# The first x tile of a gated SSM/MLP kernel: two of its five slabs by a plain load and TensorE transposes, three by one DMA transpose

## Chip, cores and metric

The kernel runs on one core of one Trainium2 chip. The metric is device microseconds (us) of one execution, the median of several runs. All tensors in memory are bf16.

## What is computed

`x` has 2048 rows of 640 features. Two branches read it and a gate mixes them.

```
g = sigmoid((x * gate_w).sum(-1))              # one number a row
a = 2 * Re(C h_t) + x * Dskip                  # h_t = Lam_bar * h_(t-1) + B_bar x_t, complex, 640 states
b = gelu(x @ w1 + b1) @ w2 + b2                # 640 -> 1728 -> 640
out = g * a + (1 - g) * b
```

`Lam_bar` and `B_bar` come from `Lambda`, `log_dt` and `B`, all per state. The recurrence over 2048 rows is done by the kernel in blocks of 256 rows.

## The kernel before

**Tiles.** The 2048 rows are cut into four x tiles of 512 rows. Products that contract over features need x with features on the partitions: `xT[q]` is `[128, 5, 512]`, five slabs of 128 features each. Gate and skip need the rows on the partitions: `xn` is `[128, 4, 640]`, two buffers used in turn. Before the change every `xT` comes by a DMA transpose out of memory (`xtrans`, L345, by `load_T`, L328, whose DMA is issued at L332) and every `xn` by a plain load (`xnload`, L336, by `load`, L323, whose DMA is issued at L325).

**Stages on TensorE.** For each x tile: the first MLP product (`m1_first` for the first eight hidden blocks of tile 0, L598; `m1` for all others, L618; a tail of 64 hidden units, L636), the SSM input product (`bproj`, L658), and per 128 rows the second MLP product (L745, tail L759) and the SSM output product (`cproj`, L791). ScalarE empties the PSUM banks (GELU at L607, L625 and L645, copies at L667, L773, L802). VectorE builds the SSM's tables at the start (L460, fed by `cols`), then scans (L698), computes the gates (L575) and combines (L460, L810).

**The opening.** `m1_first` (L591) runs slab by slab over the features: k = 0 for hidden blocks 0 to 6, then k = 1 for blocks 0 to 6, the left-over k = 0 of block 7 and k = 1 of block 7, then k = 2, 3 and 4 for all eight blocks. That is 40 matmuls of 128x128 by 512, all eight PSUM banks open at once. A matmul of slab k needs slab k of `xT[0]` and block k of W1 (`w1_k`, 128 rows by 1024 columns, 256 KB). Block 0 of W1 is loaded from ScalarE's queue, the others from SyncE's (SP's). Ahead of them TensorE runs a warm-up of eight matmuls on a zeroed tile `wz` (L400), which VectorE clears (L393).

A small transpose `cols` on TensorE (L410) turns 29 rows of parameters into columns. Everything that VectorE does for the SSM's tables starts from its copy (`cols1`, L415). It needs the identity matrix `ident`, which VectorE makes out of an iota of GpSimd (L383 to L386).

**What sets the order.** Each operation is given to a planner (`Sched.order`, L43) with an engine, an assumed duration, dependencies by name and a priority; lower goes first among those that the planner takes for ready. The result is one fixed order for each engine, and the emitter adds the semaphore waits. Operations on SP have no dependencies except the stores, so SP issues its loads in the order of `prio`: at the start the DMA transpose of slab 0, that of slabs 1 and 2, W1 blocks 1 and 2, the transpose of slabs 3 and 4, W1 blocks 3 and 4, the rest of W1 (`w1_r`), then B (two transposes), `xT[1]`, `gwb`, `xn[0]`, W2 and so on.

Of the kernel before, what the change touches and what calls it, by code (L numbers as in the profile page):

```python
# [9 lines left out]
BF16 = mybir.dt.bfloat16  # L10
# [137 lines left out]
class Prog:  # L148
# [8 lines left out]
    def op(self, name, eng, dur, reads, writes, fn, prio=None, lat=0.0, after=()):  # L157
        deps = {}
        for k in reads:
            for w in self.last_w.get(k, ()):  # L160
                deps[w.idx] = w
        for k in writes:
            for w in self.last_w.get(k, ()):
                deps[w.idx] = w
            for r in self.last_r.get(k, ()):
                deps[r.idx] = r
        for a in after:
            deps[a.idx] = a
        deps = list(deps.values())
        E = self.E  # L170

        def run(eg, deps=deps, eng=eng, fn=fn):
            E.wait(eng, *[d.done for d in deps if not (eng == "pe" and d.eng == "pe")])
            return fn()

        it = self.sch.add(name, eng, dur, deps, run, prio=prio, lat=lat)
        for k in writes:
            self.last_w[k] = [it]
            self.last_r[k] = []
        for k in reads:  # L180
            self.last_r.setdefault(k, []).append(it)
        return it


def bass_gated_mix__ssm_conv_s5__dense_activation_gelu__prompt_kernel(
# [18 lines left out]
    _, S, D = A_x.shape  # L204
# [3 lines left out]
    KD = D // 128  # L208
# [13 lines left out]
    x2 = A_x[0]  # L222
# [3 lines left out]
    with ExitStack() as es:  # L226

        def SB(name, shape, dt):
            return es.enter_context(nc.sbuf_tensor(name, list(shape), dt))

        xT = [SB(f"xT_{i}", [128, KD, 512], BF16) for i in range(NQ)]
        xn = [SB(f"xn_{i}", [128, 4, D], BF16) for i in range(2)]
# [9 lines left out]
        cols = SB("cols", [128, 3 * KP + NF], FP32)  # L242
# [10 lines left out]
        ident = SB("ident", [128, 128], BF16)  # L253
# [33 lines left out]
        PS = [es.enter_context(nc.psum_tensor(f"ps{i}", [128, 512], FP32)) for i in range(8)]  # L287
# [13 lines left out]
        op = pr.op  # L301

        def inc(eng, ins):
            return E.inc(eng, ins, eng + "_s")

        def dma_inc(eng, ins, sem):
            SEM(sem)
            E.count.setdefault(sem, 0)
            ins.then_inc(sems[sem], 16)
            E.count[sem] += 16  # L310
            return (sem, E.count[sem])
# [11 lines left out]
        def load(name, eng, sem, dst, src, writes, prio, dur=0.5, lat=2.5, reads=(), **kw):  # L323
            def fn():
                return dma_inc(eng, engines[eng].dma_start(dst, src), sem)  # L325
            return op(name, eng, dur, reads, writes, fn, prio=prio, lat=lat)

        def load_T(name, sem, pairs, writes, prio, dur, lat=3.0):  # L328
            def fn():
                t = None  # L330
                for dst, src in pairs:
                    t = dma_inc("sp", nc.sync.dma_start_transpose(dst, src), sem)  # L332
                return t
            return op(name, "sp", dur, (), writes, fn, prio=prio, lat=lat)

        def xnload(q, eng, prio=None):  # L336
            load(f"xn{q}", eng, f"l_xn{q}", xn[q % 2][:, :, :],
                 x2[q * 512:(q + 1) * 512, :].rearrange("(c p) d -> p c d", p=128),
                 [("xn", q % 2, 0), ("xn", q % 2, 1)], prio, dur=1.0, lat=6.0)
# [5 lines left out]
        def xtrans(q, ks, prio, dur):  # L345
            load_T(f"xT{q}_{ks[0]}", f"l_xT{q}_{ks[0]}", [(xT[q][:, ks[0]:ks[-1] + 1, :], x2[q * 512:(q + 1) * 512, ks[0] * 128:(ks[-1] + 1) * 128])],
                   [("xT", q, k) for k in ks], prio, dur)

        def w1load(k, eng, prio):
            load(f"w1_{k}", eng, f"l_w1{k}", W1sb[:, k, 0:FW], B_w1[k * 128:(k + 1) * 128, 0:FW], [("w1", k)], prio=prio, lat=2.6)  # L350

        w1load(0, "act", -101)
        xtrans(0, [0], 0, 1.27)
        xtrans(0, [1, 2], 1, 1.27)
        w1load(1, "sp", 2)
        w1load(2, "sp", 3)
        xtrans(0, [3, 4], 4, 1.27)
        w1load(3, "sp", 5)
        w1load(4, "sp", 6)
        load("w1_r", "sp", "l_w1r", W1sb[:, :, FW:F], B_w1[:, FW:F].rearrange("(k p) f -> p k f", p=128), [("w1", "r")], prio=20, lat=5.0)  # L360

        ROWS = {"lre": (0, A_Lambda_re), "lim": (KP, A_Lambda_im), "ldt": (2 * KP, A_log_dt), "b1a": (3 * KP, B_b1[0:nmain])}
# [24 lines left out]

        op("const", "dve", 0.8, ["iota"], ["ident"], f_const, prio=-65)

        wz = SB("wz", [128, 512], BF16)  # L390

        def f_wz():
            return inc("dve", nc.vector.memset(wz[:, :], 0.0))  # L393

        op("wz", "dve", 0.35, (), ["wz"], f_wz, prio=-70)

        def f_warm():
            t = None
            for _ in range(8):
                t = nc.tensor.matmul(PS[6][:, :], wz[:, 0:128], wz[:, :], start=True, stop=True)  # L400
            return inc("pe", t)

        op("warm", "pe", 3.2, ["wz"], [("bank", 6)], f_warm, prio=-1000)

        XT = {q: [("xT", q, k) for k in range(KD)] for q in range(NQ)}

# [2 lines left out]
        def f_cols():  # L409
            return inc("pe", nc.tensor.transpose(psC, rows[:, :], ident[:, :]))  # L410

        op("cols", "pe", 0.3, list(ROWS) + ["b1b", "ident"], [("bank", 7)], f_cols, prio=7.5)

        def f_cols1():
            return inc("dve", nc.vector.tensor_copy(out=cols[:, :], in_=psC[:, 0:RT + 1]))  # L415
# [129 lines left out]
            load_T(f"B{ci}", f"l_B{ci}", [(BT[:, ci, :, :], src)], [("BT", ci)], prio=30 + ci, dur=4.1)  # L545
        xtrans(1, range(KD), 32, 3.4)
        load("gwb", "sp", "l_gwb", gwb[:, :], gate_w.partition_broadcast(128), ["gwb"], prio=32.2)
        xnload(0, "sp", prio=32.4)
        load("w2a", "sp", "l_w2a", W2sb[:, 0:NF - 1, :], B_w2[0:nmain, :].rearrange("(j p) d -> p j d", p=128), ["w2a"], prio=33, lat=8.0)
        load("w2b", "sp", "l_w2b", W2sb[0:FL, NF - 1, :], B_w2[nmain:F, :], ["w2b"], prio=34, lat=4.0)  # L550
        load("w2c", "sp", "l_w2c", W2sb[64:64 + FL, NF - 1, :], B_w2[nmain:F, :], ["w2c"], prio=34.2, lat=4.0)
# [396 lines left out]
```

## Time and profile before

| What | Value |
|---|---|
| Median of 3 runs | 214.99 us (214.9, 214.99, 215.65) |
| Profiled execution | 215.15 us, of it the span of the profile 213.8 us |
| TensorE (PE) busy | 210.0 us, 98% of the span |
| VectorE (DVE) busy | 188.3 us, 88% |
| ScalarE (ACT) busy | 112.9 us, 53% |
| Read from memory, written | 7.63 MB, 2.62 MB |
| First matmul of the warm-up | 1.20 us |
| First and last matmul of `m1_first` (L598) | starts 4.82 us; the next stage's first (L618) starts 14.51 us |

Times in the profile count from the start of the span. PE is a matmul, PEld the load of its weights, SPq and ACTq the queues in which those engines issue DMAs; L12 is line 12 of the kernel. The time of a DMA issue in the timeline is the time that the queue spent on issuing; when the data landed is a number of its own. A matmul's duration includes its way through the array, and consecutive ones overlap: the distance from one start to the next tells the rate.

### The profile page before, as it was taken

Reading aid. Unit: us, or ns where it says so; the run is one execution under the profiler, and the core shown is the slowest. Engines: PE = TensorE matmul, PEld = TensorE weight load, DVE = VectorE, ACT = ScalarE, POOL = GpSimd, SP = SyncE. Lnnn points to the kernel's source line nnn. Section 1 sums busy time; section 2 is a strip of 40 time slices with the busy share of each in tenths; the row PEclk is TensorE's granted clock in tenths of the full one; section 3 lists DMA queues with packets and bytes.
Section 4 is the critical chain, followed back from the end, with each engine's and each line's share of the span. In section 5 each row is a group of like instructions: output and inputs, shape, how many; then the busy total and the mean of one; then the engine's idle time right before and its main releaser. Section 6 shows DMA issues by size and latency. Waiting matters only on the chain.

```text
span 213.8 us, 3098 instructions
## 1 busy us (share of the span) xinstructions
PE 210.0 (98%) x1257; PEld 119.3 (56%) x1257; DVE 188.3 (88%) x260; ACT 112.9 (53%) x205; POOL 2.5 (1%) x10
## 2 busy tenths in 40 slices
PE   7999999999999999999999999999999999999995
PEld 2344444444567675444467767444446777677673
DVE  1599999999999899999999999499999999988612
ACT  2569556679525334557835332556786554535230
POOL 1000000000000100000000010000000000000000
PEclk9999999999999999999999999999999999999999
DMA  7999699999000140000000023000000010000011
GB/s 138 297 271 192 142 364 271 224 191 204 0 0 3 61 153 3 31 0 0 0 3 31 0 49 138 32 0 0 3 0 2 0 34 31 31 34 31 31 34 31
DMA packets 30874, 16.35 MB, mean 76 GB/s; under 512 B 23948, under 2 KB 29964, under 8 KB 30860
## 3 DMA queue, kind: packets, MB, share of 16 engines
q1 hardware_dynamic: 30368, 14.57, 28.7%
q0 software_dynamic: 288, 1.31, 2.0%
q10 hardware_dynamic: 204, 0.27, 0.5%
q8 instruction: 10, 0.16, 0.4%
q14 instruction: 4, 0.03, 0.0%
HBM read 7.63 MB, written 2.62 MB: 48 GB/s over the span
## 4 chain that ended last, share of the span: by engine, by line
PE 95%; DMA 2%; SPq 1%; DVE 0%; issue 0%
PE ps L745 26%; PE ps L618 22%; PE ps L791 21%; PE ps L658 20%; PE ps L598 3%; DMA W1sb<-in_B_w_dram 2%; PE ps L759 1%; SPq L332 1%; PE ps L636 1%; DVE osb L824 0%
## 5 line engine op out<-in xcount | busy, mean ns | idle before, releaser
L745 PE MATMUL ps<-W2sb,Gl 128*128 128x320 bf16 x416 | 59.1, 299 | 0.0
L745 PEld LDWEIGHTS ps<-W2sb,Gl 128*128 128x128 bf16 x416 | 40.6, 98 | 16.5 <-ACT Gl L625 0.4
L618 PE MATMUL ps<-xT,W1sb 128*128 128x512 bf16 x220 | 48.1, 379 | 0.0
L791 PE MATMUL ps<-CT,H 128*128 128x320 bf16 x320 | 46.1, 299 | 0.0
L698 DVE TENSOR_TENSOR_SCAN W<-atab,V 128x1280 bf16<-128x1280 f32 x16 | 44.3, 2811 | 0.3
L658 PE MATMUL ps<-xT,BT 128*128 128x512 bf16 x200 | 43.8, 379 | 0.0
L773 ACT ACTIVATE E<-ps,g1col 128x320 bf16<-128x320 f32 x32 | 16.1, 526 | 42.2 <-PE ps L759 18.3
L791 PEld LDWEIGHTS ps<-CT,H 128*128 128x128 bf16 x320 | 30.7, 98 | 13.5 <-issue 1.8
L618 PEld LDWEIGHTS ps<-xT,W1sb 128*128 128x128 bf16 x220 | 21.5, 98 | 25.9
L625 ACT ACTIVATE Gl<-ps,cols 128x512 bf16<-128x512 f32 x44 | 29.7, 691 | 11.5 <-PE ps L618 11.5
L658 PEld LDWEIGHTS ps<-xT,BT 128*128 128x128 bf16 x200 | 19.4, 98 | 23.5 <-ACT Gl L625 0.4
L667 ACT ACTIVATE U<-ps 128x512 bf16<-128x512 f32 x40 | 23.6, 595 | 15.7 <-PE ps L658 15.6
L802 ACT ACTIVATE E<-ps,gcol 128x320 bf16<-128x320 f32 x30 | 15.7, 528 | 16.7 <-PE ps L791 16.6
L732 ACT ACTIVATE ps<-b2b 128x320 f32<-128x320 bf16 x32 | 14.0, 440 | 0.9
L460 DVE TENSOR_TENSOR osb<-xg,E 128x640 bf16<-128x640 bf16 x15 | 7.3, 487 | 7.8 <-ACT E L802 6.8
L810 DVE SCALAR_TENSOR_TENSOR xg<-xn,gcol,dsk 128x640 bf16<-128x640 bf16 x16 | 13.8, 882 | 0.4
L575 DVE SCALAR_TENSOR_TENSOR scr<-xn,gwb 128x640 bf16<-128x640 bf16 x16 | 13.2, 823 | 0.4
L460 DVE TENSOR_TENSOR H<-H,V 128x1280 bf16<-128x1280 bf16 x16 | 12.5, 821 | 0.3
L460 DVE TENSOR_TENSOR V<-V,W 128x1280 bf16<-128x1280 bf16 x16 | 12.5, 821 | 0.3
L460 DVE TENSOR_TENSOR V<-mr,U 128x2560 bf16<-128x2560 bf16 x8 | 11.9, 1489 | 0.2
L460 DVE TENSOR_TENSOR H<-c,W 128x2560 bf16<-128x2560 bf16 x8 | 11.9, 1488 | 0.1
L460 DVE TENSOR_TENSOR V<-s,W 128x2560 bf16<-128x2560 bf16 x8 | 11.9, 1484 | 0.0
(77 smaller groups left out, 101.2 us busy)
## 6 DMA issues: line engine op xcount, KB each, us to landing
out_dram<-osb SPq DMA_DIRECT2D x15, 160.0 KB, 1.8
W2sb<-in_B_w_dram SPq DMA_DIRECT2D x1, 2080.0 KB, 12.2
xn<-in_A_x_dram SPq DMA_DIRECT2D x2, 640.0 KB, 6.4
xn<-in_A_x_dram POOLq DMA_DIRECT2D x2, 640.0 KB, 4.8
W1sb<-in_B_w_dram SPq DMA_DIRECT2D x4, 256.0 KB, 4.1
W1sb<-in_B_w_dram SPq DMA_DIRECT2D x1, 880.0 KB, 6.1
W1sb<-in_B_w_dram ACTq DMA_DIRECT2D x1, 256.0 KB, 2.8
gwb<-in_gate_w_dram SPq DMA_DIRECT2D x1, 160.0 KB, 5.2
```

What stands on the lines that cost most here:

```text
L460: return inc("dve", nc.vector.tensor_tensor(out=o, in0=a, in1=b, op=o_))
L618: t = nc.tensor.matmul(PS[bank][:, :], W1sb[:, k, jf * 128:(jf + 1) * 128], xT[q][:, k, :], start=(k == 0), stop=(k == KD - 1))
L625: return inc("act", nc.scalar.activation(Gl[q % 2][:, jf, :], PS[bank][:, :], ACT.Gelu_apprx_tanh, bias=b1col[:, jf:jf + 1]))
L658: t = nc.tensor.matmul(PS[bank][:, :], BT[:, ci, kd, k * 128:(k + 1) * 128], xT[q][:, kd, :], start=(kd == 0), stop=(kd == KD - 1))
L667: return inc("act", nc.scalar.activation(dst, src, ACT.Copy, scale=1.0 if ci == 0 else -1.0))
L698: t = inc("dve", nc.vector.tensor_tensor_scan(out=g[:, ci, :], data0=a, data1=v[:, ci, :], initial=0.0, op0=ALU.mult, op1=ALU.add))
L732: return inc("act", nc.scalar.activation(PS[bank][:, 0:HALF], b2b[:, cols], ACT.Copy))
L745: t = nc.tensor.matmul(PS[bank][:, 0:HALF], Gl[q % 2][:, jf, t4 * 128:(t4 + 1) * 128], W2sb[:, jf, cols], start=False, stop=False, skip_gr ...
L773: return inc("act", nc.scalar.activation(E1[c % NE][:, cols], PS[bank][:, 0:HALF], ACT.Copy, scale=g1col[:, c:c + 1]))
L791: t = nc.tensor.matmul(PS[bank][:, 0:HALF], H[b % NHB][:, ci, k, s * 128:(s + 1) * 128], CT[:, ci, k, cols], start=(i == 0), stop=(i == 2 ...
L802: return inc("act", nc.scalar.activation(E2[c % NE][:, cols], PS[bank][:, 0:HALF], ACT.Copy, scale=gcol[:, c:c + 1]))
L810: return inc("dve", nc.vector.scalar_tensor_tensor(out=xg[c % 2][:, :], in0=xn[q % 2][:, c % 4, :], scalar=gcol[:, c:c + 1], in1=dsk[:, :] ...
```

## The change

Slabs 0 and 1 of the first x tile no longer come by DMA transpose. A plain load `xna` on SP brings their 256 features, rows on the partitions, into the first 256 columns of `xn[0]`. TensorE transposes them, four 128x128 blocks to a slab (`xt0`, `xt1`, into banks 7 and 6 as bf16), and VectorE copies each result into `xT[0]` (`xc0`, `xc1`). Slabs 2 to 4 come by one DMA transpose, now behind W1 blocks 1 and 2. The later load of `xn[0]` brings only the other 384 features (`xnb`).

The warm-up becomes six matmuls instead of eight, on a constant 1.0 read with stride 0 that exists before the kernel starts, so that `wz` and its clearing fall away. One more matmul on that constant with 192 columns (`fill`) stands behind the transposes. `cols` goes behind the ninth matmul of `m1_first` by priority (9.5), where it was behind the seventh (7.5).

```diff
+        KN = 2
         w1load(0, "act", -101)
-        xtrans(0, [0], 0, 1.27)
-        xtrans(0, [1, 2], 1, 1.27)
-        w1load(1, "sp", 2)
-        w1load(2, "sp", 3)
-        xtrans(0, [3, 4], 4, 1.27)
-        w1load(3, "sp", 5)
-        w1load(4, "sp", 6)
+        load("xna", "sp", "l_xna", xn[0][:, :, 0:KN * 128], x2[0:512, 0:KN * 128].rearrange("(c p) d -> p c d", p=128), ["xna"], 0, dur=0.5, lat=2.0)
+        w1load(1, "sp", 1)
+        w1load(2, "sp", 2)
+        xtrans(0, range(KN, KD), 3, 1.8)
+        w1load(3, "sp", 4)
+        w1load(4, "sp", 5)
...
-        wz = SB("wz", [128, 512], BF16)
-
-        def f_wz():
-            return inc("dve", nc.vector.memset(wz[:, :], 0.0))
-
-        op("wz", "dve", 0.35, (), ["wz"], f_wz, prio=-70)
+        one = nc.const_aps.tensor(1.0, [128, 1], BF16)

         def f_warm():
             t = None
-            for _ in range(8):
-                t = nc.tensor.matmul(PS[6][:, :], wz[:, 0:128], wz[:, :], start=True, stop=True)
+            for _ in range(6):
+                t = nc.tensor.matmul(PS[5][:, :], one.broadcast_to([128, 128]), one.broadcast_to([128, 512]), start=True, stop=True)
             return inc("pe", t)

-        op("warm", "pe", 3.2, ["wz"], [("bank", 6)], f_warm, prio=-1000)
+        op("warm", "pe", 2.5, (), [("bank", 5)], f_warm, prio=-1000)
+
+        for k in range(KN):
+            bank = 7 - k
+            pt = PS[bank][:, :].bitcast(BF16)[:, 0:512]
+
+            def f_xt(k=k, pt=pt):
+                t = None
+                for c in range(4):
+                    t = nc.tensor.transpose(pt[:, c * 128:(c + 1) * 128], xn[0][:, c, k * 128:(k + 1) * 128], ident[:, :])
+                return inc("pe", t)
+
+            op(f"xt{k}", "pe", 0.44, ["xna", "ident"], [("bank", bank)], f_xt, prio=-990 + k)
+
+            def f_xc(k=k, pt=pt):
+                return inc("dve", nc.vector.tensor_copy(out=xT[0][:, k, :], in_=pt))
+
+            op(f"xc{k}", "dve", 0.42, [("bank", bank)], [("xT", 0, k)], f_xc, prio=-2000 + k)
+
+        def f_fill():
+            return inc("pe", nc.tensor.matmul(PS[5][:, 0:192], one.broadcast_to([128, 128]), one.broadcast_to([128, 192]), start=True, stop=True))
+
+        op("fill", "pe", 0.16, (), [("bank", 5)], f_fill, prio=-980)
...
-        op("cols", "pe", 0.3, list(ROWS) + ["b1b", "ident"], [("bank", 7)], f_cols, prio=7.5)
+        op("cols", "pe", 0.3, list(ROWS) + ["b1b", "ident"], [("bank", 7)], f_cols, prio=9.5)
...
-        xnload(0, "sp", prio=32.4)
+        load("xnb", "sp", "l_xnb", xn[0][:, :, KN * 128:D], x2[0:512, KN * 128:D].rearrange("(c p) d -> p c d", p=128),
+             [("xn", 0, 0), ("xn", 0, 1)], 32.4, dur=1.0, lat=6.0, reads=["xna"])
```

## The prediction

> **What bounds the kernel now.** I read the chain of work that ended last first, then its pieces in order of time. The page gives the chain's shares:
>
> ```profile
> PE 95%; DMA 2%; SPq 1%; DVE 0%; issue 0%
> ```
>
> The chain in order of time shows where it is not TensorE:
>
> ```profile
> 2.03 1.29 SPq L332
> 3.32 0.05 issue
> 3.37 3.89 DMA W1sb<-in_B_w_dram
> 7.26 0.14 issue
> 7.39 7.28 PE ps L598 x33
> 14.67 5.40 PE ps L618 x25
> ...
> 211.61 0.55 DVE osb L824
> ```
>
> From 7.39 us on it is matmuls without a gap until the last copy. What ends last before that is the landing of W1 block 1, issued at 3.37 because two transpose issues stand ahead of it on SP. So the opening alone can move, and each us by which L618 starts earlier or later is a us of the whole. The timeline of the opening:
>
> ```profile
> 0.87 0.27 DVE L393 MEMSET wz<- 128x256 uint32 x1 [0.87 <-PEq L933]
> ...
> 1.20 3.59 PE L400 MATMUL ps<-wz 128*128 128x512 bf16 x8 [1.20 <-DVE wz L393]
> ...
> 4.82 2.13 PE L598 MATMUL ps<-xT,W1sb 128*128 128x512 bf16 x7
> 5.22 0.15 PEld L598 LDWEIGHTS ps<-xT,W1sb 128*128 128x128 bf16 x1 [0.27 <-issue]
> 5.65 0.81 PEld L598 LDWEIGHTS ps<-xT,W1sb 128*128 128x128 bf16 x4 [0.28 <-issue]
> ...
> 6.79 0.22 PE L410 MATMUL ps<-ident,rows 128*128 128x128 bf16 x1
> 7.04 0.19 DVE L415 CAST cols<-ps 128x29 f32<-128x29 bf16 x1 [5.12 <-PE ps L410]
> ...
> 7.39 6.85 PE L598 MATMUL ps<-xT,W1sb 128*128 128x512 bf16 x31 [0.39 <-DMA W1sb<-in_B_w_dram]
> ```
>
> Two facts matter. Of the gap only 0.39 us is idle: seven matmuls fill 4.82 to 7.0. And weight loads stand 0.43 us apart (5.22, 5.65) until about 5.65, where matmuls also last 609 to 634 ns and afterwards 379; later 65 matmuls take 14.03 us, 0.216 each. So TensorE runs at half rate until 5.65.
>
> **What the Trainium skill says.** "TensorE: Matmul & The Clock Gate", Part 1, says the array starts at half clock and is released after sustained activity in a free-running window of about 3.4 us, typically some 4 us after the start, varying by run. The trace agrees in kind: first matmul 1.20, full rate 5.65, 4.45 us. The same page, Part 4, gives a 128x128 bf16 transpose 275 to 390 ns singly and says that transposes do not count as busy for the clock in the same way; the one transpose here took 219 ns, at full clock, and about its weight for the clock the trace says nothing. "DMA: Bandwidth & Descriptors", "Issuing engines are not separate DMA queues": SP's and ACT's DMAs share 16 engines and interleave. The trace agrees: between 2.5 and 3.0 us both queues move data, 0.05 and 0.10 MB.
>
> **The change part by part.**
>
> *Warm-up without `wz`.* The 0.27 us clearing and its wait go. SP and ACT issue first at 0.75, GpSimd at 0.74, so TensorE starts near 0.8. Six matmuls at 0.43 end near 3.4.
>
> *`xna`.* It is issued at 0.75 and lands at L. W1 block 0, of the same 256 KB and issued at the same moment, landed after 2.8 us, at 3.55, alone; its packets ran from about 1.75 to 3.15. Now both loads share the engines. W1's 128 packets took 139 ns each there (49 packets at 84.7% of 16 engines in 0.5 us), 84 ns later in deep queues; `xna` has 512 pieces of 512 B. Packets of 256 B took 18 to 22 ns; I estimate 30 for 512 B. Together (128 x 84 to 139 + 512 x 30)/16 = 1.6 to 2.1 us after 1.75, and 0.4 to the semaphore: L = 3.8 to 4.2. I take 3.9; ends 3.55 (not disturbed at all) and 4.3.
>
> *Transposes and copies.* The old slab landed at 4.75 and TensorE began at 4.82: 0.07. A cold weight load is 0.15, a quarter of a cold matmul is 0.107: I take 0.13 a transpose, and 0.25 for the first load and way through the array beyond that: 4 x 0.13 + 0.25 = 0.77 for `xt0`, bounds 0.6 and 1.0. VectorE starts 0.03 behind (7.01 to 7.04). The copy of 512 columns out of PSUM isn't in the trace. 29 columns took 0.19 and 320 (two operands, f32) 0.55, so 0.19 + 483 x 1.24 ns = 0.79 is above it; half that slope gives 0.49. I take 0.55, bounds 0.45 and 0.75. TensorE again 0.05. `m1_first` starts at S = 3.9 + 0.07 + 0.77 + 0.03 + 0.55 + 0.05 = 5.37. `xt1` (0.52) and `fill` (0.16) stand inside `xc0`'s time. `xc1` ends about 0.6 after S, wanted by the seventh matmul. Both copies lie in VectorE's idle 5.12 us ahead of L415.
>
> *SP's queue.* Three transposes with 1.23 + 1.29 + 1.23 us of issue become one load (0.5) and one transpose, which I put at 1.6: two slabs cost 1.23 to 1.29, five under a full queue 4.61. W1 block 1 is issued at 1.25 instead of 3.37. Before, SP's 1.70 MB up to W1 block 4 flowed from 2.5 to about 10.1 us, 224 GB/s. At that rate, from 1.75, with W1 block 0's 0.26 MB ahead of all: W1 block 1 lands by 5.7 (wanted near 7.0), slabs 2 to 4 by 7.4 to 8.6 (wanted near 9.1), W1 block 4 by about 10.9 at worst (wanted near 12.5). So the old bound is gone and TensorE itself is next. The issue of B and everything behind it (`w1_r`, `xT[1]`, `xnb`, W2, C) comes up to 1.9 us earlier. `xnb` and `xna` carry together what `xn[0]` did; the added wait of `xnb` is for a landing some 18 us past: nothing.
>
> *`cols` at place nine.* It used to hide in the gap; now it costs 0.1 in the stream (0.05 to 0.2). It runs at about 7.4 instead of 6.79, so VectorE's tables are 0.65 later. What waits for that: the GELU table load, ended 11.23, then 11.9, with the first GELU wanted near 12.9; and the last state block, whose slack the end of the timeline shows:
>
> ```profile
> 197.72 1.56 DVE L460 TENSOR_TENSOR H<-H,V 128x1280 bf16<-128x1280 bf16 x2
> ...
> 202.43 2.89 PE L791 MATMUL ps<-CT,H 128*128 128x320 bf16 x20
> ```
>
> It is ready at 199.28 and used at 202.43: 3.15 us, far more than 0.65 plus the gain. If that cover were gone, the delay would count in full.
>
> *The sum.* With full clock at 5.65 as before: 0.28 us from S are at half rate, 0.65 of a matmul; the other 39.35 at 0.216 take 8.50; plus `cols` 0.1: L618 starts at 14.25. Before it was 7.39 + 33 x 0.216 = 14.52, which agrees with its 14.51. Gain 0.26 us. The profiled execution (213.8 span and 1.35 around it, 215.15) would become 214.89; it lies 0.16 above the median, so the median becomes 214.73, and I say 214.7. With all good ends (L 3.55, 0.6, 0.45) S is 4.75 and the gain 0.58; with all bad ends (4.3, 1.0, 0.75, 0.2) S is 6.2 and the loss about 0.55. This case's own range is 214.4 to 215.5.
>
> The removal sounds larger than it is: W1 block 1 comes 2 us earlier, but the seven half-clock matmuls under that wait were useful work, and now they start later.
>
> **Rivals.**
>
> *The clock comes late (slower).* The place is TensorE between the warm-up's end at 3.4 and S. There it idles about 0.5 us and then only transposes for about 1.2 us. Before, it was busy all of 1.20 to 5.65. If that stretch fails the activity test, the release waits for another window, 5.65 + 3.41 (the page's figure) = 9.06 at worst. Then 3.69 us from S hold 8.6 matmuls, 31.4 take 6.78, `cols` 0.1: L618 at 15.94, a loss of 1.4, 216.4 us. For: the skill's sentence on transposes, and the shorter warm-up. Against: a window which is half full may do, and `fill` and the weight loads also work the array. Each us of delay past S costs 0.49 us (1 - 0.216/0.43); it is a loss from about 6.2 and passes 0.5% from about 8.1. A release halfway, at 7.3, gives 215.5.
>
> *The clock comes early (faster).* TensorE starts 0.4 us sooner. If release follows the start, or comes at the least time of 3.4 us, it is there by 4.3 to 5.2. With L at 3.55 and S at 4.75 all 40 matmuls run full: 4.75 + 8.64 + 0.1 = 13.49, gain 1.0, 214.0 us. Against: everything must go well.
>
> *The slabs are late.* If three slabs in one transpose take longer than the bytes say (the first two calls before issued 393 KB at 0.75 and landed it at 5.83), k = 2 waits at 9.1 for a landing near 10, 215.6 us. Against: a slack of 0.5 to 1.7. That the change does not do what it says is hardly possible here: the priorities alone order SP's first loads.
>
> **How the numbers follow.** Likeliest case 0.58 (214.7), late clock 0.22 (216.4 in full, 215.5 halfway), early clock 0.14 (214.0), late slabs 0.06 (215.6). A measurement of this kernel tells about 0.5%, 1.07 us, from no change: below 213.9 is faster, above 216.1 slower. Slower gets a little over half of the late clock, 0.12, and 0.01 of the slabs. Faster gets a third of the early clock, 0.05. The rest, 0.82, is within. The range leaves out those ends, 0.18: 213.9 to 216.1.
>
> **What would show it.** Right: the first warm-up matmul near 0.8; transposes near 4.0; L598 from about 5.4 with no idle until L618 at about 14.25; W1 block 1 landed well before its first use. Late clock: L598 weight loads 0.43 us apart past 6.5. Late slabs: an idle gap of L598 on xT near 9 us. The prediction is wrong if L618 starts before 13.4 or after 15.6, or if a wait of TensorE appears later than that, on VectorE or on a load.

## The result and the profile after

| | Before | Changed |
|---|---|---|
| Median | 215.31 us (214.9 to 215.65, 4 runs) | 217.03 us (216.84 to 217.41, 4 runs) |
| Span of the profiled execution | 213.8 us | 215.5 us |

The ratio is 1.0083, 95% interval 1.0056 to 1.011: slower by 1.7 us, above the range. A ratio compares all runs with runs of the kernel before from the same occasion, so it can differ a little from the ratio of two medians. (One more run of the kernel before was made beside the changed one; hence 215.31 instead of 214.99.)

The changed kernel's shares of the chain that ended last say that TensorE still sets the end:

```profile
PE 97%; DMA 2%; DVE 0%; issue 0%
```

Its opening in the timeline (start, duration, engine, line; in brackets the idle time before it and what ended it; L395 is now the warm-up, L407 the x transposes, L413 their copies, L616 the first MLP stage, L636 the next):

```profile
0.78 2.72 PE L395 MATMUL ps<-const-bfloat16-1.0 128*128 128x512 bf16 x6 [0.78 <-PEq L951]
...
4.76 0.77 PEld L407 LDWEIGHTS ps<-ident,xn 128*128 128x128 bf16 x8 [2.17 <-DMA xn<-in_A_x_dram]
4.76 1.03 PE L407 MATMUL ps<-ident,xn 128*128 128x128 bf16 x8 [1.27 <-DMA xn<-in_A_x_dram]
5.41 0.85 DVE L413 COPY xT<-ps 128x512 bf16<-128x512 bf16 x2 [3.49 <-PE ps L407]
...
5.89 3.74 PE L616 MATMUL ps<-xT,W1sb 128*128 128x512 bf16 x9
6.29 0.15 PEld L616 LDWEIGHTS ps<-xT,W1sb 128*128 128x128 bf16 x1 [0.28 <-issue]
...
8.85 0.15 PEld L616 LDWEIGHTS ps<-xT,W1sb 128*128 128x128 bf16 x1 [0.28 <-issue]
...
9.52 6.85 PE L616 MATMUL ps<-xT,W1sb 128*128 128x512 bf16 x31
...
16.21 1.03 PE L636 MATMUL ps<-xT,W1sb 128*128 128x512 bf16 x4
```

Read it in this order. The wait for W1 block 1 is gone, as the change meant it. A wait of 1.27 us for the plain x load has come, and it stands earlier, between warm-up and transposes. After it, weight loads are 0.43 us apart up to 8.85: nine matmuls and `cols` take 3.63 us, 5.89 to 9.52, and eight of the nine run at half rate, where before the half rate ended soon after 5.65. The last 31 take 6.69 us, 0.216 each, as ever. The next stage starts at 16.21 instead of 14.51, 1.70 later, and the span is 1.7 longer: the whole loss lies in the opening, and everything behind it is only shifted.

The two first loads, issued at 0.74 and 0.75, landed after (the last column, us from issue to landing):

```profile
xn<-in_A_x_dram SPq DMA_DIRECT2D x1, 256.0 KB, 4.0
W1sb<-in_B_w_dram ACTq DMA_DIRECT2D x1, 256.0 KB, 3.3
```

So the theory had two links: the x load lands late because W1 block 0 is moved at the same time, and the idle time that this leaves on TensorE keeps it at half clock. The rivals: the transposes are what keeps the clock down, and SP's queue is late by itself.

### The profile page after: what moved, and what is told of

It is laid out like the page before. It is cut to its first block, busy times and chain, and to the rows that moved or that the text cites. A ratio compares the mean times of both kernels' runs of the same rounds, so it can differ in the third digit from the quotient of the medians.

```text
span 215.5 us, 3110 instructions
## 1 busy us (share of the span) xinstructions
PE 211.2 (98%) x1264; PEld 120.2 (56%) x1264; DVE 188.6 (88%) x261; ACT 113.3 (53%) x205; POOL 2.5 (1%) x10
## 4 chain that ended last, share of the span: by engine, by line
PE 97%; DMA 2%; DVE 0%; issue 0%
PE ps L763 26%; PE ps L636 22%; PE ps L809 21%; PE ps L676 20%; PE ps L616 5%; DMA xn<-in_A_x_dram 2%; PE ps L777 1%; PE ps L654 1%; PE ps L407 0%; DVE osb L842 0%; PE ps L418 0%; PE ps L427 0%
## 5 line engine op out<-in xcount | busy, mean ns | idle before, releaser
L636 PE MATMUL ps<-xT,W1sb 128*128 128x512 bf16 x220 | 48.1, 379 | 0.0
L636 PEld LDWEIGHTS ps<-xT,W1sb 128*128 128x128 bf16 x220 | 21.5, 98 | 26.0
L820 ACT ACTIVATE E<-ps,gcol 128x320 bf16<-128x320 f32 x30 | 15.8, 528 | 17.9 <-PE ps L809 17.9
L477 DVE TENSOR_TENSOR W<-mi,U 128x2560 bf16<-128x2560 bf16 x8 | 11.9, 1485 | 0.0
```

The source lines that it names most:

```text
L477: return inc("dve", nc.vector.tensor_tensor(out=o, in0=a, in1=b, op=o_))
L636: t = nc.tensor.matmul(PS[bank][:, :], W1sb[:, k, jf * 128:(jf + 1) * 128], xT[q][:, k, :], start=(k == 0), stop=(k == KD - 1))
L820: return inc("act", nc.scalar.activation(E2[c % NE][:, cols], PS[bank][:, 0:HALF], ACT.Copy, scale=gcol[:, c:c + 1]))
```

## Experiments on the clock

**Fill the gap.** Three more warm-up matmuls in the changed kernel.

```diff
-            for _ in range(6):
+            for _ in range(9):
```

> The changed kernel with nine warm-up matmuls instead of six, so that TensorE is busy from 0.78 to about 4.6 and the idle time of 1.36 us before the first transpose is filled; the transposes stay as they are. Theory (the idle time is what delayed full clock): full clock by about 5.7 as in the kernel before, slab work starts at 5.9 as in the changed kernel, L636 starts near 14.6, so 1.6 us under the changed kernel and 0.1 us over the one before, ratio to before 1.000 to 1.002. Rival (transposes do not count, or something else delays it): matmuls still 0.43 us apart until about 9, L636 near 16.2, ratio 1.008.

Measured: 215.34 us, ratio 1.0002 (0.9994 to 1.0011). Its timeline:

```profile
3.72 0.15 PEld L395 LDWEIGHTS ps<-const-bfloat16-1.0 128*128 128x128 bf16 x1 [0.28 <-issue]
4.46 0.45 PEld L407 LDWEIGHTS ps<-ident,xn 128*128 128x128 bf16 x8 [0.59 <-DMA xn<-in_A_x_dram]
4.47 0.62 PE L407 MATMUL ps<-ident,xn 128*128 128x128 bf16 x8
...
14.34 3.40 PE L636 MATMUL ps<-xT,W1sb 128*128 128x512 bf16 x15
```

Full clock is there before the transposes, whose eight take 0.62 us instead of 1.03. Three matmuls that compute nothing win back the whole 1.7 us, by the ratio over 13 runs. (In this profile the x load landed at 4.42, 0.3 us sooner than in the changed kernel's, which is part of its earlier L636.) The loss was the clock, and the idle time made it.

**Make the gap in the kernel before.** Five warm-up matmuls instead of eight.

```diff
-            for _ in range(8):
+            for _ in range(5):
```

> The kernel before with five warm-up matmuls instead of eight: nothing else is changed, TensorE idles from about 3.5 to 4.8 and there are no x transposes on it. Theory (the idle time is what delayed full clock): full clock only at about 9.1 to 9.3; of the matmuls after 7.4 some 3 more run at half rate and the seven before it end near 7.9, so L618 starts near 15.6 to 15.8 instead of 14.5, ratio to before 1.005 to 1.006. Rival (the transposes delayed it): no change, L618 at 14.5, ratio 1.000.

Measured: 216.31 us, ratio 1.0048 (1.0031 to 1.0065). The timeline of this kernel, with no x transpose in it:

```profile
4.74 3.17 PE L598 MATMUL ps<-xT,W1sb 128*128 128x512 bf16 x7 [1.23 <-DMA xT<-in_A_x_dram]
...
9.09 0.15 PEld L598 LDWEIGHTS ps<-xT,W1sb 128*128 128x128 bf16 x1 [0.28 <-issue]
9.42 5.93 PEld L598 LDWEIGHTS ps<-xT,W1sb 128*128 128x128 bf16 x28 [0.18 <-issue]
15.46 2.04 PEld L618 LDWEIGHTS ps<-xT,W1sb 128*128 128x128 bf16 x10
15.68 2.10 PE L618 MATMUL ps<-xT,W1sb 128*128 128x512 bf16 x9
```

1.23 us of idle, and half rate until about 9.3, much as in the changed kernel; L618 at 15.68, within the expected 15.6 to 15.8. The loss is smaller than 1.7 because part of the slow work hides under the wait for W1 block 1. The same effect without any transpose: they are not its cause.

**Fill that gap with transposes.** The same five, and then eleven transposes of the zeroed tile.

```diff
-            for _ in range(8):
+            for _ in range(5):
...
+        def f_warmt():
+            t = None
+            for _ in range(11):
+                t = nc.tensor.transpose(PS[6][:, :].bitcast(BF16)[:, 0:128], wz[:, 0:128], ident[:, :])
+            return inc("pe", t)
...
```

> The kernel before with five warm-up matmuls and then eleven 128x128 transposes of the zeroed tile instead of the last three, about 1.4 us of them, so that TensorE has no idle time before its first slab. If transposes count as activity for the clock: as before, L618 at 14.5, ratio 1.000. If they do not count: the same as with five matmuls and an idle gap, full clock at about 9.1 to 9.3, ratio 1.005 to 1.006.

Measured: 215.21 us, ratio 0.9998 (0.999 to 1.0006). The last half-rate weight load and the next stage in its timeline (its lines L606 and L626 are L598 and L618):

```profile
6.79 0.15 PEld L606 LDWEIGHTS ps<-xT,W1sb 128*128 128x128 bf16 x1 [0.28 <-issue]
...
14.73 2.97 PE L626 MATMUL ps<-xT,W1sb 128*128 128x512 bf16 x13
```

Transposes do not act as idle time does: half rate ended near 7.0, not 9.3, and all 13 runs lie below the lowest of the six with the gap. It was later than 5.65, and a release before about 7 is hidden by the wait for W1 block 1 in this kernel, so whether a transpose weighs as much as a matmul stays open.

**Start sooner.** The kernel before with its warm-up on the constant, nine matmuls from 0.78.

```diff
...
-            for _ in range(8):
-                t = nc.tensor.matmul(PS[6][:, :], wz[:, 0:128], wz[:, :], start=True, stop=True)
+            for _ in range(9):
+                t = nc.tensor.matmul(PS[6][:, :], one.broadcast_to([128, 128]), one.broadcast_to([128, 512]), start=True, stop=True)
...
```

> The kernel before with the warm-up on the constant: it starts at about 0.78 instead of 1.20 and has nine matmuls, to about 4.6. If full clock comes a fixed time (4.45 us) after the start of unbroken work, half rate ends at about 5.2; if it comes at the edge of a window that runs free from launch, it ends at 5.65 as before. Either way the time is that of the kernel before within 0.1 us, ratio 1.000, since W1 block 1 still bounds the opening at 7.4.

Measured: 215.32 us, ratio 1.0009 (0.9997 to 1.002): no change, as expected. Half rate ended near 5.4 in its profile, between the two expectations. Later runs speak against a fixed time: two kernels with these same nine matmuls from 0.78 were at full rate by 4.6 in their profiles, and with the same start half rate ended before 3.74 in one profile and only after 6.62 in another (below). A window whose edge falls differently from run to run fits that, as the Trainium skill has it ("TensorE: Matmul & The Clock Gate", Part 1); no run here shows the window itself. The page puts the spread at half a microsecond either way around some 4 us; from the first matmul to full rate these profiles show from under 3.0 to about 6.0 us.

## Experiments on the loads

**The x load without its rival.** W1 block 0 on SP behind it, and one more warm-up matmul.

```diff
-        w1load(0, "act", -101)
...
+        w1load(0, "sp", 0.5)
         w1load(1, "sp", 1)
...
-            for _ in range(6):
+            for _ in range(7):
```

> The changed kernel with W1 block 0 on SP directly behind the x load instead of on ScalarE's queue beside it, and seven warm-up matmuls (to about 3.8). Theory A (the x load landed at 4.7 because W1 block 0 shared the engines with it): the load lands near 3.6 to 3.9, the gap is gone, slab work starts near 4.9, L636 near 14.0 to 14.3, ratio to before 0.997 to 0.999. Theory B (SP's queue starts its first transfer late by itself): it lands at 4.3 or later, a gap of 0.5 us or more stays, L636 at 14.5 to 16.2 according to when full clock comes, ratio 1.000 to 1.008.

Measured: 214.87 us, ratio 0.9976 (0.9963 to 0.999). The issue of the x load and its landing:

```profile
xn<-in_A_x_dram SPq DMA_DIRECT2D x1, 256.0 KB, 3.0
```

It lands at 3.77, 0.95 us sooner, on the same queue: theory A. In this profile half rate went on until after 6.62 and L636 started at 14.54, later than I expected; yet the median is better than before.

```profile
3.81 1.04 PE L407 MATMUL ps<-ident,xn 128*128 128x128 bf16 x8
...
6.62 0.15 PEld L616 LDWEIGHTS ps<-xT,W1sb 128*128 128x128 bf16 x1 [0.28 <-issue]
```

The transposes show no idle time before them, for the seventh warm-up matmul lasts until 3.92. So full clock can come late without an idle gap too, here some 3 us later than in the earliest profile (the last one below). Idle time is not the only thing that decides when it comes.

**The two loads exchanged.**

```diff
-        w1load(0, "act", -101)
-        load("xna", "sp", "l_xna", xn[0][:, :, 0:KN * 128], x2[0:512, 0:KN * 128].rearrange("(c p) d -> p c d", p=128), ["xna"], 0, dur=0.5, lat=2.0)
+        w1load(0, "sp", 0)
+        load("xna", "act", "l_xna", xn[0][:, :, 0:KN * 128], x2[0:512, 0:KN * 128].rearrange("(c p) d -> p c d", p=128), ["xna"], -101, dur=0.5, lat=2.0)
...
-            for _ in range(6):
+            for _ in range(7):
```

> The changed kernel with the two first loads exchanged: the x load on ScalarE's queue, W1 block 0 first on SP, seven warm-up matmuls. Theory A (the engines are shared): the x load still lands at 4.1 to 4.7 and the time is 1.002 to 1.008 of before. Theory B (ScalarE's queue moves its first packets sooner than SP's): the x load lands near 3.6, L636 near 14.0 to 14.3, ratio 0.997 to 0.999.

Measured: median 215.12 us, ratio 1.002 (1.0001 to 1.0038). The x load took 3.9 us on ScalarE's queue too: theory A again, and B has fallen. Its 22 runs fall into two groups, 14 from 214.91 to 215.33 and 8 from 216.25 to 217.28, with nothing between; the median of the whole says little here. The idle time is 0.73 us:

```profile
4.65 0.45 PEld L407 LDWEIGHTS ps<-ident,xn 128*128 128x128 bf16 x8 [1.64 <-DMA xn<-in_A_x_dram]
4.65 0.62 PE L407 MATMUL ps<-ident,xn 128*128 128x128 bf16 x8 [0.73 <-DMA xn<-in_A_x_dram]
```

This profile is of the first group, at full clock by 4.65. That the other group met the late clock is inferred from its times, which are close to those of the changed kernel; no profile of it was taken.

**One edit alone.** W1 block 0 moved as above, with the change's own six warm-up matmuls.

> The changed kernel with one edit alone: W1 block 0 on SP behind the x load, and the six warm-up matmuls of the change. The x load lands near 3.7 as in the run with seven, slab work starts near 4.9, and TensorE idles about 0.3 us between warm-up and transposes. Theory (full clock is granted at the edge of a free-running window if the window was nearly all busy): 0.3 us of idle is small enough in most or all runs, median 214.5 to 215.2, at most a few runs near 216. Rival (any idle time starts the wait afresh at 3.75): full clock not before 7.2, all runs from 215.2 up, median 215.5 to 216.

Measured: 214.56 us (214.22 to 215.0, 16 runs), ratio 0.9974 (0.9964 to 0.9984), faster than both kernels. Its timeline:

```profile
3.73 0.77 PEld L407 LDWEIGHTS ps<-ident,xn 128*128 128x128 bf16 x8 [1.14 <-DMA xn<-in_A_x_dram]
3.74 1.04 PE L407 MATMUL ps<-ident,xn 128*128 128x128 bf16 x8 [0.24 <-DMA xn<-in_A_x_dram]
4.46 0.15 PEld L418 LDWEIGHTS ps<-const-bfloat16-1.0 128*128 128x128 bf16 x1
...
4.86 1.19 PEld L616 LDWEIGHTS ps<-xT,W1sb 128*128 128x128 bf16 x7 [0.25 <-DVE xT L413]
...
6.57 0.11 PEld L616 LDWEIGHTS ps<-xT,W1sb 128*128 128x128 bf16 x2 [0.51 <-DMA W1sb<-in_B_w_dram]
...
7.49 0.22 PE L427 MATMUL ps<-ident,rows 128*128 128x128 bf16 x1 [0.32 <-DMA rows<-in_B_b_dram]
...
14.24 2.97 PE L636 MATMUL ps<-xT,W1sb 128*128 128x512 bf16 x13
```

An idle time of 0.24 us, and full clock between 4.46 and 4.86, with the transposes before it. The rival, a wait that starts afresh at 3.75, wanted 7.2 and has fallen. The price is small: W1 block 1, now third on SP, lands at 6.52 instead of 5.35, and the first matmul that needs it starts 0.18 us late, with its weight load at 6.57. From +0.83% to -0.26% by the place of one load.

**Is the new path needed?** The kernel before with the early warm-up and W1 block 1 ahead of the transpose of slabs 1 and 2, without x transposes on TensorE.

```diff
-        xtrans(0, [1, 2], 1, 1.27)
-        w1load(1, "sp", 2)
+        w1load(1, "sp", 1)
+        xtrans(0, [1, 2], 2, 1.27)
```

> The kernel before with the early warm-up of nine matmuls on the constant, and with W1 block 1 issued ahead of the transpose of slabs 1 and 2; no x transposes on TensorE. Theory (the order of SP's loads alone made the gap at 7.0 to 7.4): block 1 lands near 5.7 and slab 1 near 6.4, L598 runs from 4.6 to 4.8 without idle, L618 starts near 13.9 to 14.1, ratio to before 0.997 to 0.998. Rival (slab 1 takes the place of block 1 as the late one): a gap stays before the second slab, L618 at 14.4 to 14.6, ratio 0.999 to 1.001.

Measured: 215.24 us, ratio 1.0 (0.9988 to 1.0013). The number is the rival's, but its mechanism is not: TensorE waited 0.79 us, to 7.04, for the parameter rows of `cols`, which neither theory had named:

```profile
7.04 0.22 PE L405 MATMUL ps<-ident,rows 128*128 128x128 bf16 x1 [0.79 <-DMA rows<-in_B_b_dram]
```

So that was moved as well, to the fourteenth place (priority 14.5, and a longer assumed landing of the rows, which the planner needs to place it there).

> The kernel before with the early warm-up, W1 block 1 issued ahead of the transpose of slabs 1 and 2, and the parameter transpose (cols) behind the fourteenth instead of the seventh matmul of the first stage. With block 1 ahead alone, TensorE waited 0.8 us for the parameter rows at the seventh place. Theory (that wait had taken the place of the wait for block 1): L598 now runs from about 4.6 without idle, L618 starts at 13.8 to 14.1, ratio to before 0.996 to 0.998. Rival (slab 1 lands late as well): an idle gap before the second slab of 0.3 us or more, ratio 0.999 to 1.001.

Measured: 215.04 us, ratio 1.0 (0.9989 to 1.0012): now the rival is right. The wait of TensorE in this kernel's timeline:

```profile
6.72 1.68 PE L593 MATMUL ps<-xT,W1sb 128*128 128x512 bf16 x7 [0.49 <-DMA xT<-in_A_x_dram]
```

Slab 1 by DMA transpose lands at 6.7 there. Reordering SP's loads alone wins nothing. What the plain load brings sooner is slab 1: with W1 block 0 moved, both slabs had landed at 3.69 and the copy of slab 1 ended at 5.23.

**Once more, on top of the best.** The version with W1 block 0 moved, and `cols` at place fourteen.

```diff
-        op("cols", "pe", 0.3, list(ROWS) + ["b1b", "ident"], [("bank", 7)], f_cols, prio=9.5)
+        op("cols", "pe", 0.3, list(ROWS) + ["b1b", "ident"], [("bank", 7)], f_cols, prio=14.5)
```

> The changed kernel with W1 block 0 behind the x load on SP, six warm-up matmuls, and the parameter transpose (cols) behind the fourteenth matmul of the first stage instead of the ninth. With W1 block 0 moved alone, TensorE waited 0.32 us at the ninth place for the parameter rows. Theory (that wait is the last idle time in the opening): it goes, L636 starts near 13.9 to 14.1 when full clock is there by 5 us, ratio to before 0.995 to 0.997, at best 0.3 us under the version with block 0 moved alone. Rival (W1 block 1 or the VectorE copy of the parameters holds the next matmul instead, or the tables come too late): the same time as with block 0 moved alone or slower, ratio 0.997 to 1.000.

Measured: 215.02 us, ratio 0.9988 (0.998 to 0.9996): a miss. The 0.32 us wait for the rows is gone, and the three slabs hold slab 2's first matmul instead:

```profile
3.74 0.62 PE L407 MATMUL ps<-ident,xn 128*128 128x128 bf16 x8 [0.24 <-DMA xn<-in_A_x_dram]
...
8.45 5.79 PE L616 MATMUL ps<-xT,W1sb 128*128 128x512 bf16 x25 [0.51 <-DMA xT<-in_A_x_dram]
```

Why its median is also above that of the version without this edit isn't settled: its profile is not longer (span 213.4 against 213.6), the two were measured on different occasions, and the planner moved other work as well. It is not a version to prefer.

## Why the prediction was wrong

**The landing of `xna` was mis-sized.** The prediction took L = 3.9 with ends 3.55 and 4.3; it was 4.71. It added up packets, set all sixteen engines to work at 1.75 and let them end together. The packets were near the forecast: 128 of 140 ns and 512 of 27 ns make 1.98 us of sixteen engines, inside its 1.6 to 2.1. But they ran from 1.80 to 4.31, 2.5 us. The engines moved 106 GB/s from 1.75 to 2.0 and 131 up to 2.25, against 353 from 3.25 to 3.75. Nor did they end together: packets of W1 block 1 moved from 3.57 on, while the last ones of x were still to come, and the sixteen updates of the x load's semaphore arrived from 3.93 to 4.72. Of block 0's 128 packets 107 began before 3.0, of the x load's 512 only 40. A sign of it stood in the profile before: block 0 and the first transpose were both issued at 0.75, and the one moved from 1.77, the other only from 2.52. From there on block 0 was not alone, as the prediction read it.

**The likeliest case kept full clock at 5.65; it came near 9.2.** The step that failed is the sentence that the idle time is about 0.5 us and that a window half full may do. The idle time was 1.27, because L was late. The late clock had a chance of 0.22 and should have been the main case at that L: an idle time of 0.24 left all 16 runs at 215.0 or less, 0.73 appears to have slowed 8 of 22, 1.27 slowed all four and 1.23 at least five of six (each idle time is that of one profile). Its reason was half wrong: I gave the transposes as an argument for it, and the runs with the gap alone and with transposes in its place show that idle time does it. What puts full clock off in a run without idle time, as in the profile with the x load ahead and seven warm-up matmuls, stays open.

**The sum with the measured terms closes.** From the forecast 14.25: L and the start of TensorE behind it 0.79, less 0.15 for transposes that took 0.65 until the copy (forecast 0.80) and 0.12 for copy and start, 0.48 (forecast 0.60), leaves S at 5.89, +0.52. Nine matmuls and `cols` took 3.63 us; at full rate they would be 2.04, and 0.14 of the slow rate was in the forecast, +1.45. Together 16.22; measured 16.21. The late clock's forecast loss of 1.4 is short of the measured 1.70 by the later S.

**What was right.** The first matmul at 0.78 and the warm-up's end near 3.4. The wait for W1 block 1 is gone: issued at 1.26, landed at 5.35. Slabs 2 to 4 were issued at 2.27 and landed 5.2 us later, at 7.5, inside 7.4 to 8.6, though the issue took 2.1 instead of 1.6. `cols` ran 2.7 us later than before (9.46 against 6.79) and nothing waited for its tables. The shift behind the opening is one constant.

**The gain itself.** With the load in order the change gives 0.26%, some 0.56 us: more than the likeliest case's 0.26 us, less than the early clock's 1.0. In its profile S was 4.87 and full clock came before it; but that profile is of one of its slower runs, and L636 at 14.24 is only 0.27 earlier than before.

## What to carry to other kernels

A warm-up has to reach the first real work: leave about a microsecond of idle time behind it and the array is paid for at half rate long after, and three empty matmuls can be worth 1.7 us, as here. Full clock can still come late in a single run. Before you move an input to a path with its own arrival, work out what else is in flight in those first microseconds, and let the load that TensorE waits for go alone and first. When a wait is removed from an opening, name the next arrival in order: here the parameter rows, slab 1, W1 block 1 again and the three slabs took its place in one version or another.

## What the runs showed that I had not expected

- Two loads of 256 KB issued within 0.01 us on SP's and ScalarE's queues do not land together: W1 block 0 after 3.0 to 3.3 us, the x load after 3.7 to 4.0, whichever queue each is on (three profiles); with W1 block 0 behind it on its own queue the x load takes 2.9 to 3.0. Why the x load comes second each time isn't settled; its pieces are 512 B and W1's 2 KB.
- Half rate ended between 3.0 us (before 3.74) and about 6 us (after 6.62) from the same first matmul at 0.78, in different profiles with at most 0.24 us of idle time behind the warm-up.
- A matmul whose operands are one constant with stride 0 keeps the ordinary pace, 0.43 us at half rate.
- VectorE copies 512 bf16 columns out of PSUM in 0.42 us, below the bounds' low end of 0.45.
